# Attention and FFN on one core: an opening emitted step by step, with some of its work on other engines

## The chip, the core and the metric

The kernel runs on one core of a Trainium2 chip. The metric is the device time of one execution in microseconds (us). Five engines run their own instruction streams in order and wait for each other by semaphores: TensorE (PE; its weight loads are PEld), VectorE (DVE), ScalarE (ACT), GpSimd (POOL), and SyncE (SP), which here issues most of the DMAs. A line such as L166 is a line of the kernel.

## The reference

```
k_p = k.reshape(B, H, S // 8, 8, D).mean(axis=3);  v_p likewise     # B=8, H=8, S=576, D=64
scores = q @ k_p.T / 8;  attn = softmax(scores);  x = attn @ v_p
x -> (B, S, 512)
xn = (x - mean) / sqrt(var + 1e-6) * g_ln
out = x + relu(xn @ w_ch1) @ w_ch2                                    # 512 -> 2048 -> 512
```

All of it is float32. Keys and values are averaged over eight neighbours before the attention, so each query sees 72 keys.

## The kernel before

The 4608 tokens are cut into 36 tiles of 128, and four tiles make a chunk (nine chunks, c = 0 to 8). A tile has a stage A (load the queries, `scores`, `probs`) and a stage B (`values`: attention output x, its row statistics, the centred and scaled z, and z's split and transpose). A chunk then has the input half of the FFN (`ffn_in`, 16 feature blocks f, hidden values in `ring`) and the output half (`ffn_out`, L765), in two halves over the features and four tiles each.

The FFN runs in f16 with every f32 factor split in a high and a low part, and three products for each factor pair. For that the weights have to be prepared once. W1 and W2 come as 8 blocks each of 128 x 1024 values. For each block `convert` (C) takes a maximum on VectorE (L195), two passes on ScalarE (L198, L202) and one on VectorE (L205). `max_w1` and `max_w2` (M1, M2) turn four blocks' maxima into a scale by way of a small product on TensorE (L149). `split_w` (S) then writes the high part on ScalarE (L161) and the low part on VectorE (L166).

The opening (`START`) prepares the weights and does chunks 0 and 1. Batch 0's and batch 1's keys and values are pooled by products with a banded matrix (L356, L372); later batches' on GpSimd (L299 to L303, L313 to L315). Chunk 0 turns its probabilities and z by products on TensorE (L484, L491, L504), later chunks by DMA. From chunk 2 on the input half uses seven products in place of eight on sums of W1's blocks (`sums_w` T, `sum_last` U: L272 to L276 and L259, L260) and of z.

`START` is a list of steps, traced in that order. The instructions of each engine are then ordered by the framework's scheduler, which runs its own model of the engines' times. So the list sets priorities, not the order in which an engine executes. Buffers: three PSUM tiles for FFN results (`ps_f`), one each for scores, values and small products (`ps_m`); weight blocks land in `tsp`, `ring` and `raw`, keys in two `kr` buffers, values in two `vr` buffers, and a load waits until its buffer is free.

Of the kernel before, what the change touches and what calls it, by code (L numbers as in the profile page):

```python
# [63 lines left out]
def attn_ffn_kernel(ctx: ExitStack, tc: tile.TileContext, qT, kT, v, kvn, kvt, g, w1, w2, out):  # L64
# [78 lines left out]
    def all_max(src, n=P):  # L143


        e, dst = scalar_tile("rowmax"), scalar_tile("allmax")
# [2 lines left out]
        nc.tensor.matmul(  # L149
            ps,  # L150
            lhsT=e.bitcast(BF16)[:n, 1:2].broadcast_to([n, P]),
            rhs=ident[:n, :n],
            start=True,
            stop=True,
        )
        nc.vector.tensor_reduce(out=dst, in_=ps, axis=AX.X, op=ALU.max)
        return dst

    def split(src, scale, hi, lo, shared=False):
# [6 lines left out]
        nc.vector.scalar_tensor_tensor(  # L166
# [21 lines left out]
    def convert(mat, b):  # L188
# [6 lines left out]
        nc.vector.tensor_reduce(  # L195
            out=wm[mat][:, b : b + 1], in_=hi.bitcast(F32), axis=AX.X, op=ALU.max, apply_absolute_value=True
        )
# [7 lines left out]
        nc.vector.scalar_tensor_tensor(  # L205
# [52 lines left out]
    def split_t(src, dst):  # L258
        nc.scalar.copy(out=dst[:, 0], in_=src)  # L259
        nc.gpsimd.tensor_tensor(out=dst[:, 1], in0=src, in1=dst[:, 0], op=ALU.subtract)  # L260

    def sums_w(h, k):
# [54 lines left out]
    def max_v(b):  # L317
# [12 lines left out]
    def tokens(b, n):  # L330
        if (b, n) == (1, 1):
            part = zts[:, 8:16].rearrange("p a c -> p (a c)").bitcast(F32)
            part = part.rearrange("p (i c) -> p i c", i=NTOK - 1)
            return [part[:, i] for i in range(NTOK - 1)] + [at(2, 5 * WC + NTOK * DM, 1)[:, 0]]
        x = at(*((1, 5 * WC), (2, 0), (2, 5 * WC))[2 * b + n], NTOK)
        return [x[:, i] for i in range(NTOK)]

    def load_tokens(b, n):
        x = tokens(b, n)
        if (b, n) == (1, 1):  # L340
            full = zts[:, 8:16].rearrange("p a c -> p (a c)").bitcast(F32)
        else:
            full = area[(1, 2, 2)[2 * b + n]][:, (5, 0, 5)[2 * b + n] * WC :][:, : (NTOK - 1) * DM]
        full = full.rearrange("p (i c) -> p i c", i=NTOK - 1)
        nc.sync.dma_start(out=full, in_=kvn[b, n])
        nc.sync.dma_start(out=x[NTOK - 1][: S % P], in_=kvt[b, n])
# [556 lines left out]
```

## Time and profile before

| what | value |
|---|---|
| median of 3 runs | 871.95 us (871.56 to 872.1) |
| the profiled execution | 870.89 us |
| its span, first to last instruction | 868.8 us |
| mean granted TensorE clock | 0.978 |
| PE busy in the span | 831.3 us |
| DMA, mean over the span | 101 GB/s; 355 to 383 GB/s in the first three of 40 slices |

A profile row of the timeline has start, length, engine, line, operation, output<-input, count, and in brackets the idle time of the engine before it with what ended it. A row of a group has the busy time of all its instructions, the mean of one in ns, and the idle time before them. Up to the end of chunk 1, at about 275 us, the trace shows the opening; behind it chunks 2 to 8.

### The profile page before, as it was taken

To read this page: it belongs to the slowest core of one execution; us is meant where nothing else is said; L and a number is where in the kernel's file an instruction comes from. 1 tells how busy PE (TensorE), PEld (TensorE's weight loads), DVE (VectorE), ACT (ScalarE), POOL (GpSimd) and SP (SyncE) were. 2 spreads that over 40 slices of the span, in tenths; PEclk is the share of its full clock that TensorE was granted. 3 is DMA by queue.
4 is the path that set the end of the run, shared out by engine and by line. 5 is a ranking of instruction groups with operands and counts; after the bars stand their busy time and mean duration, and the time that the engine had idled before them with its cause. 6 is when DMAs were issued, how large, how long until landed. Compare 5 with 4: busy or idle time off the path is not lost. (4 is left out here: it accounts for less than half of the span.)

```text
span 868.8 us, 14907 instructions
## 1 busy us (share of the span) xinstructions
PE 831.3 (96%) x5808; PEld 545.2 (63%) x5808; DVE 561.1 (65%) x1148; ACT 324.3 (37%) x615; POOL 294.9 (34%) x429
## 2 busy tenths in 40 slices
PE   6699896999999999999999998999999999999998
PEld 5586642444556766676676665766766676757483
DVE  4999799814486738574956485648674847494242
ACT  3797442303142424252434332523343333323140
POOL 0534688534465453255213334231111201120000
PEclk9888897999999999999999999999999999999999
DMA  9992520343346342435343414432434143221001
GB/s 355 364 383 77 124 67 7 101 99 71 88 115 170 77 98 63 123 91 121 69 115 89 101 50 123 110 63 49 116 71 65 32 115 62 38 55 55 0 2 48
DMA packets 145109, 87.35 MB, mean 101 GB/s; under 512 B 125328, under 2 KB 126480, under 8 KB 142480
## 3 DMA queue, kind: packets, MB, share of 16 engines
q1 hardware_dynamic: 143888, 85.52, 37.1%
q10 hardware_dynamic: 1152, 0.90, 0.4%
q8 instruction: 45, 0.74, 0.3%
q14 instruction: 24, 0.20, 0.1%
HBM read 45.09 MB, written 9.44 MB: 63 GB/s over the span
## 5 line engine op out<-in xcount | busy, mean ns | idle before, releaser
L765 PE MATMUL ps_f<-w,ring 128*128 128x512 f16 x1728 | 380.7, 379 | 0.0
L765 PEld LDWEIGHTS <-ring 128*128 128x128 f16 x1728 | 167.8, 98 | 193.9 <-issue 0.2
L700 PE MATMUL ps_f<-zts,w 128*128 128x256 f16 x1680 | 207.1, 273 | 3.2 <-DVE raw L721 1.5
L700 PEld LDWEIGHTS <-w 128*128 128x128 f16 x1680 | 163.3, 98 | 23.9 <-issue 2.8
L775 DVE SCALAR_TENSOR_TENSOR x<-ps_f,cy,x 128x512 f32<-128x512 f32 x72 | 53.8, 748 | 124.7 <-PE ps_f L765 122.4
L669 PE MATMUL ps_f<-zts,w 128*128 128x512 f16 (+1 forms) x480 | 96.2, 360 | 9.4 <-DVE x L775 6.6
L700 PE MATMUL ps_f<-zts,tsp 128*128 128x256 f16 x672 | 96.1, 272 | 1.5 <-DVE rowmax L127 1.2
L464 POOL TENSOR_TENSOR phl<-e,phl 128x512 f16<-128x512 f32 x32 | 37.4, 1169 | 159.5 <-ACT phl L457 159.5
L741 DVE SCALAR_TENSOR_TENSOR ring<-raw,ring 128x512 f16<-128x512 f32 x112 | 82.2, 760 | 9.0 <-ACT ring L740 8.7
L740 ACT ACTIVATE ring<-raw 128x512 f16<-128x512 f32 x112 | 64.8, 622 | 54.4 <-DVE raw L734 53.9
L669 PEld LDWEIGHTS <-w 128*128 128x128 f16 x480 | 49.3, 104 | 50.3 <-issue 16.8
L718 ACT COPY raw<-ps_f 128x256 f32<-128x256 f32 x56 | 20.8, 371 | 143.7 <-PE ps_f L700 140.8
L700 PEld LDWEIGHTS <-tsp 128*128 128x128 f16 x672 | 64.0, 98 | 12.1 <-issue 1.9
L638 POOL TENSOR_TENSOR hl<-raw,hl 128x640 f16<-128x640 f32 x28 | 41.0, 1479 | 78.9 <-ACT hl L637 43.0
L734 DVE TENSOR_TENSOR raw<-ps_f,raw 128x256 f32<-128x256 f32 x112 | 42.3, 419 | 22.4 <-PE ps_f L700 22.0
L313 POOL TENSOR_TENSOR vr<-vr 72x256 f32<-72x256 f32 x48 | 38.8, 816 | 48.3 <-DMA vr<-in_v_dram 48.2
L721 DVE TENSOR_TENSOR raw<-ps_f,raw 128x256 f32<-128x256 f32 x56 | 23.7, 424 | 45.6 <-PE ps_f L700 40.5
L453 ACT ACTIVATE e<-e 128x576 f32<-128x576 f32 x32 | 21.8, 683 | 62.6 <-DVE e L441 44.5
L427 PE MATMUL ps_a<-kblk,q 128*128 128x144 f32 (+1 forms) x320 | 44.7, 292 | 0.0
L427 PEld LDWEIGHTS ps_a<-kblk,q 128*128 128x128 f32 (+1 forms) x320 | 40.5, 183 | 5.7 <-issue 2.0
L727 DVE TENSOR_TENSOR raw<-ps_f,raw 128x256 f32<-128x256 f32 x56 | 23.6, 421 | 31.4 <-PE ps_f L700 28.5
L637 ACT CAST hl<-raw 128x640 f16<-128x640 f32 x28 | 19.2, 722 | 57.8 <-DVE a L614 26.3
(137 smaller groups left out, 1000.5 us busy)
## 6 DMA issues: line engine op xcount, KB each, us to landing
q<-in_qT_dram SPq DMA_DIRECT2D x36, 256.0 KB
out_dram<-x SPq DMA_DIRECT2D x36, 256.0 KB
tsp<-in_w_dram SPq DMA_DIRECT2D x8, 1024.0 KB
kr<-in_kT_dram SPq DMA_DIRECT2D x24, 288.0 KB
vr<-in_v_dram SPq DMA_DIRECT2D x48, 144.0 KB
raw<-in_w_dram SPq DMA_DIRECT2D x6, 1024.0 KB
w<-in_kvn_dram SPq DMA_DIRECT2D x3, 1024.0 KB
ring<-in_w_dram SPq DMA_DIRECT2D x2, 1024.0 KB
```

The costliest lines, as they stand in the source:

```text
L313: eng.tensor_add(out=vr[:, 0:4, :], in0=vr[:, 0:4, :], in1=vr[:, 4:8, :])
L427: nc.tensor.matmul(ps[r, p // 2, p % 2 * 2 * KV : (p % 2 + 1) * 2 * KV], lhsT=q[:, p, r], rhs=kblk[b % NKB][:, p, :], start=True, stop=True,)
L464: nc.gpsimd.tensor_tensor(out=ph[:, 0, :, KA:P], in0=e[:, :, 0:KA], in1=ph[:, 0, :, 0:KA], op=ALU.subtract)
L638: nc.gpsimd.tensor_tensor(out=zhl[:, 1, :], in0=src, in1=zhl[:, 0, :], op=ALU.subtract)
L669: nc.tensor.matmul(ps, lhsT=w[:, part, fs], rhs=zT[:, kz, cols], start=(n == 0), stop=(n == 3 * NKT - 1),)
L700: nc.tensor.matmul(ps, lhsT=w[:, part, f * P : (f + 1) * P], rhs=z, start=start and n == 0, stop=stop and n == 3 * KH - 1, skip_group_chec ...
L721: nc.vector.tensor_tensor(out=cc[:, 0, :HC], in0=m2, in1=cc[:, 0, :HC], op=ALU.add)
L734: nc.vector.tensor_tensor(out=cc[:, j, HC:], in0=u3, in1=cc[:, j, HC:], op=ALU.add)
L740: nc.scalar.activation(out=hh[:, 0, f], in_=cc[:, j], func=AF.Relu)
L741: nc.vector.scalar_tensor_tensor(out=hh[:, 1, f], in0=cc[:, j], scalar=0.0, in1=hh[:, 0, f], op0=ALU.max, op1=ALU.subtract)
L765: nc.tensor.matmul(ps, lhsT=h[:, part, i, cols], rhs=w[:, wp, j], start=(n == 0), stop=(n == 3 * NFT // 2 - 1),)
L775: nc.vector.scalar_tensor_tensor(out=x, in0=ps, scalar=out_scale(c, tt, half), in1=x, op0=ALU.mult, op1=ALU.add)
```

## The change

Every operation of the opening becomes a generator that yields where another engine's result is wanted next. `START` now has 574 steps, each naming an operation that is advanced by one piece, and the region runs under `manual_schedule`, so that each engine executes its instructions in exactly the order in which the pieces emit them. Behind the opening the scheduler orders as before. With it, six things move:

- W2's maxima (`MAXM`): in place of VectorE's maximum a ScalarE pass over the converted block writes the sum of absolute values, which bounds the maximum.
- W2's first four low parts (`LO_POOL`): ScalarE scales the block once more in place, and GpSimd subtracts over 128 x 1024.
- Chunk 0's z (`parts_turned`): x is turned by four f32 products, and a fifth product with the negated identity takes the mean off in PSUM; ScalarE reads it twice with z's scale (high part, and all of z), and GpSimd subtracts (`Z_LO`). VectorE's z (L567) and its low part (L507) are gone for chunk 0.
- Chunk 1's z is computed by GpSimd.
- Batch 1's keys and values are pooled on GpSimd like those of the later batches (HK.1, HV.1), from loads into `kr` and `vr`.
- Batch 0's keys (K0) are summed by VectorE from a load in the later batches' layout. Small memsets of `split_v` go to GpSimd.

```diff
+MAXM = {1: "dve", 2: "act"}
+LO_POOL = ((2, 0), (2, 1), (2, 2), (2, 3))
+Z_LO = "pool"
 START = """
-LD K0 A.0 C.1.0 V0 R.2.0 R.2.1 C.1.1 A.1 C.1.2 B.0 C.1.3 M1.0 S.1.0 S.1.1 S.1.2 S.1.3 R.2.2 R.2.3 B.1 A.2 I.0.0.0 ...
+LN.2 LN.2 LK.0 LK.0 LK.1 LK.1 Q.0 Q.0 R.1.0 R.1.0 R.1.1 R.1.1 Q.1 Q.1 R.1.2 R.1.2 LG LG HK.1.0 A.0 R.1.3 R.1.3 HV.1.0
...
-    def split(src, scale, hi, lo, shared=False):
+    def split(src, scale, hi, lo, pool=False):
         nc.scalar.activation(out=hi, in_=src, func=AF.Copy, scale=scale)
-        if shared:
-            nc.gpsimd.tensor_scalar_mul(out=src, in0=src, scalar1=scale)
+        if pool:
+            nc.scalar.activation(out=src, in_=src, func=AF.Copy, scale=scale)
+            yield
             nc.gpsimd.tensor_tensor(out=lo, in0=src, in1=hi, op=ALU.subtract)
             return
+        yield
         nc.vector.scalar_tensor_tensor(
...
+        if MAXM[mat] == "act":
+            yield
+            nc.scalar.activation(
+                out=lo.bitcast(F32), in_=w, func=AF.Abs, accum_out=wm[mat][:, b : b + 1]
+            )
...
-    def parts_turned(z, dst):
-        ps = psum["ps_f"].tile([P, CH], F32, name="ps_f")
+    def parts_turned(x, ln, cv, dst):
+        ps = psum["ps_m"].tile([P, CH], F32, name="ps_m").rearrange("p (k c) -> p k c", k=NKT)
         for k in range(NKT):
-            nc.tensor.transpose(out=ps[:, k * P : (k + 1) * P], in_=z[:, k * P : (k + 1) * P], identity=identf)
-        ps = ps.rearrange("p (k c) -> p k c", k=NKT)
-        nc.scalar.copy(out=dst[:, 0:NKT], in_=ps)
-        nc.vector.tensor_tensor(out=dst[:, NKT:], in0=ps, in1=dst[:, 0:NKT], op=ALU.subtract)
+            nc.tensor.matmul(ps[:, k], lhsT=x[:, k * P : (k + 1) * P], rhs=identf, start=k == 0, ...)
+        nc.tensor.matmul(ps, lhsT=ln[:, 0:1].broadcast_to([P, P]), rhs=minus.unsqueeze(1).broadcast_to([P, NKT, P]), ...)
+        yield
+        scale = cv[:, 1:2]
+        nc.scalar.activation(out=dst[:, 0:NKT], in_=ps, func=AF.Copy, scale=scale)
+        if Z_LO == "pool":
+            z = wk1.tile([P, DM], F32, name="z").rearrange("p (k c) -> p k c", k=NKT)
+            nc.scalar.activation(out=z, in_=ps, func=AF.Copy, scale=scale)
+            yield
+            nc.gpsimd.tensor_tensor(out=dst[:, NKT:], in0=z, in1=dst[:, 0:NKT], op=ALU.subtract)
+            return
...
-        nc.vector.tensor_scalar(
+        (nc.gpsimd if c < 2 else nc.vector).tensor_scalar(
             out=z, in0=x, scalar1=ln[:, 0:1], scalar2=ln[:, 2:3], op0=ALU.subtract, op1=ALU.mult
         )
...
     def first_k():
-        pool_tokens_k(0)
+        for i in range(2):
+            if i:
+                yield
+            kr = k_first[:, 2 * i : 2 * i + 2]
+            nc.vector.tensor_add(out=kr[:, :, 0:4], in0=kr[:, :, 0:4], in1=kr[:, :, 4:8])
+            nc.vector.tensor_add(out=kr[:, :, 0:2], in0=kr[:, :, 0:2], in1=kr[:, :, 2:4])
+            for j in range(2):
...
-    for token in START.split():
-        name, *args = token.split(".")
-        ops[name](*map(int, args))
+    begun = {}
+    with tc.manual_schedule():
+        for token in START.split():
+            if token not in begun:
+                name, *args = token.split(".")
+                begun[token] = iter(ops[name](*map(int, args)) or ())
+            next(begun[token], None)
+        for steps in begun.values():
+            all_of(steps)
```

The lines shift: L166 becomes L211, L205 becomes L264, L195 becomes L248 (W1 only), L161 is L204, L765 is L882.

VectorE before, from the scale of W1's first half (`gs`) on; `w_91` is W1, `w_92` W2, `x` and `z` are tiles 0 and 1:

```order
L231 TENSOR_SCALAR gs<-g_sb,s_323 128x4
L546 TENSOR_TENSOR x<-ps_a,rs 128x512
L557 BN_STATS st<-x 128x6
L166 SCALAR_TENSOR_TENSOR w_91<-w_91,gs 128x1024
L558 BN_AGGR ln<-st 128x2
L536 TENSOR_SCALAR sm<-ps_a,cv 128x8
L567 TENSOR_SCALAR z<-x,ln 128x512
L544 RECIPROCAL rs<-sm 128x8
L546 TENSOR_TENSOR x<-ps_a,rs 128x512
L166 SCALAR_TENSOR_TENSOR w_91<-w_91,gs 128x1024
L557 BN_STATS st<-x 128x6
L507 TENSOR_TENSOR zts<-ps_f,zts 128x4x128
```

VectorE in the change at the same place:

```order
L297 TENSOR_SCALAR gs<-g_sb,s_320 128x4
L264 SCALAR_TENSOR_TENSOR w_91<-w_91,ring 128x1024
L511 TENSOR_REDUCE mx<-ps_a 128x8
L264 SCALAR_TENSOR_TENSOR w_92<-w_92,raw 128x1024
L211 SCALAR_TENSOR_TENSOR w_91<-w_91,gs 128x1024
L264 SCALAR_TENSOR_TENSOR w_91<-w_91,ring 128x1024
L211 SCALAR_TENSOR_TENSOR w_91<-w_91,gs 128x1024
L641 TENSOR_SCALAR sm<-ps_a,cv 128x8
L649 RECIPROCAL rs<-sm 128x8
L651 TENSOR_TENSOR x<-ps_a,rs 128x512
```

z and its low part are gone from VectorE, the low parts of W1 stand between conversions, and tile 0's x now stands ahead of `gs`.

GpSimd before, from the last probabilities of chunk 0 (`pt`) to tile 4's (`phl`); `kr` and `kblk` are keys of batch 2:

```order
L497 TENSOR_TENSOR pt<-phl_116,pt 72x512 x2
L456 MEMSET phl_116 128x8x40
L299 TENSOR_TENSOR kr<-kr 128x288
L300 TENSOR_TENSOR kr<-kr 128x144
L303 TENSOR_TENSOR kblk_113<-kr 64x72 x4
```

GpSimd in the change, from the low part of tile 3's z (L605) to W2's first low parts (L208):

```order
L605 TENSOR_TENSOR zts<-z,zts 128x4x128
L385 TENSOR_TENSOR vr<-vr 72x256
L386 TENSOR_TENSOR vr<-vr 72x128
L387 TENSOR_TENSOR vp<-vr 72x64
...
L371 TENSOR_TENSOR kr<-kr 128x288
L372 TENSOR_TENSOR kr<-kr 128x144
L375 TENSOR_TENSOR kblk_113<-kr 64x72 x2
L208 TENSOR_TENSOR w_92<-w_92 128x1024
```

W2's low parts stand behind all of batch 1's value heads (`vr`), its key pairs and one key pair of batch 2.

SP before, from W1's last two blocks of the first half (`ring`) on:

```order
L186 DMA ring<-in_w_dram 128x2048 x2
L419 DMA q<-in_qT_dram 128x512
L186 DMA raw<-in_w_dram 128x2048 x2
L345 DMA w_92<-in_kvn_dram 128x2048
L346 DMA w_92<-in_kvt_dram 64x512
```

SP in the change, from W2's second block (`raw`) on:

```order
L231 DMA raw<-in_w_dram 128x2048
L366 DMA kr<-in_kT_dram 128x576
L379 DMA vr<-in_v_dram 72x512
L231 DMA tsp_93<-in_w_dram 128x2048
L366 DMA kr<-in_kT_dram 128x576
L493 DMA q<-in_qT_dram 128x512
L231 DMA tsp_94<-in_w_dram 128x2048
L379 DMA vr<-in_v_dram 72x512
L231 DMA raw<-in_w_dram 128x2048
```

Loads of weight blocks now alternate with loads into the two key and two value buffers.

More of the change, by code (lines that the diff above doesn't have):

```diff
@@ L328, in at, with tokens, load_tokens @@
         return area[m][:, lo : lo + n * DM].rearrange("p (i c) -> p i c", i=n)
[L330 to L346, printed above, removed]
+    def tokens(n):
+        if n == 1:
+            part = zts[:, 8:16].rearrange("p a c -> p (a c)").bitcast(F32).rearrange("p (i c) -> p i c", i=NTOK - 1)
+            return part, at(2, 5 * WC + NTOK * DM, 1)[:, 0]
+        x = at(*((2, 5 * WC), None, (1, 5 * WC))[n], NTOK)
+        return x[:, : NTOK - 1], x[:, NTOK - 1]
+    def load_tokens(n):
+        full, last = tokens(n)
+        nc.sync.dma_start(out=full, in_=kvn[n])
+        nc.sync.dma_start(out=last[: S % P], in_=kvt[n])
     def token_tiles():
@@ L367, in pool_tokens_v @@
     def pool_tokens_v(b):
-        x = tokens(b, 1)
+        full, last = tokens(2 if b == 0 else 1)
+        x = [full[:, i] for i in range(NTOK - 1)] + [last]
         ps = psum["ps_m"].tile([P, DM], F32, name="ps_m")[:KV]
@@ new lines, in probs_turned @@
+        for n in range(4):
+            h = 4 * i + n
+            nc.tensor.matmul(
+                ps[:, n],
+                lhsT=kblk[0][:, h // 2, h % 2 * KV : (h % 2 + 1) * KV],
+                rhs=q[:, h // 2],
+                start=True,
+                stop=False,
+            )
+            nc.tensor.matmul(
+                ps[:, n], lhsT=mx[:, h : h + 1].broadcast_to([P, KV]), rhs=minus, start=False, stop=True
+            )
+        yield
+        hs = slice(4 * i, 4 * i + 4)
+        nc.scalar.activation(out=et[:KV, hs], in_=ps, func=AF.Exp, scale=EXP_SCALE)
@@ L515, in values @@
             cv = scalar_tile("cvm", 3)
-            for r, b in segs:
-                nc.vector.tensor_copy(out=cv[r], in_=CV[b][r])
         pt = PT.pop(t)
@@ L535, in values @@
                 )
+        yield
+        if len(segs) > 1:
+            for r, b in segs:
+                nc.vector.tensor_copy(out=cv[r], in_=CV[b][r])
         nc.vector.tensor_scalar(
@@ L566, in values @@
         Z[t] = ln
-        nc.vector.tensor_scalar(
+        if not seven:
+            yield
+        nc.gpsimd.tensor_copy(out=ln[:, 2:4], in_=cv[:, 1:3])
+        if c == 0:
+            zTs[c] = zts[:, c * 8 : (c + 1) * 8]
+            yield
+            yield from parts_turned(x, ln, cv, zTs[c][:, :, tt * P : (tt + 1) * P])
+            return
+        if seven:
+            yield
+        (nc.gpsimd if c < 2 else nc.vector).tensor_scalar(
             out=z, in0=x, scalar1=ln[:, 0:1], scalar2=ln[:, 2:3], op0=ALU.subtract, op1=ALU.mult
@@ L784, in stage_a, with stage_b @@
             load_q(t + 2)
-        scores(t)
-        probs(t)
-    def stage_b(t):
-        values(t)
-        transpose_z()
+            yield
+        yield from scores(t)
+        if t >= TPC:
+            yield
+            yield from probs(t)
+    def stage_b(t, turn=True):
+        yield from values(t)
+        if turn and t >= TPC:
+            yield
+            transpose_z()
     def prep_k(b, parts=range(NPAIR)):
```

251 lines of the change are left out of this document (166 added, 85 removed).

## The prediction, made before the run

> **What bounds the kernel now.** I read the busy row and the slices of the page first, then busy time by stretches, then TensorE's timeline.
>
> ```profile
> PE 831.3 (96%) x5808; PEld 545.2 (63%) x5808; DVE 561.1 (65%) x1148; ACT 324.3 (37%) x615; POOL 294.9 (34%) x429
> DVE  4999799814486738574956485648674847494242
> ```
> ```profile
> 20.00:50.00 30.00, 20.37 (x165) 17.10 (x164) 29.33 (x54) 24.63 (x30) 12.04 (x16) 0.77 1.02 366
> 50.00:105.00 55.00, 49.80 (x406) 39.41 (x405) 50.23 (x111) 38.45 (x58) 27.03 (x38) 0.88 0.56 185
> 105.00:164.00 59.00, 51.37 (x266) 24.53 (x264) 56.26 (x71) 21.21 (x31) 49.54 (x46) 0.91 0.20 44
> ```
> ```profile
> 180.00:200.00 20.00, 20.00 (x98) 9.75 (x97) 5.70 (x9) 3.59 (x7) 1.28 (x2) 1.00 0.32 85
> ```
>
> The columns of a stretch are its length, then busy time of PE, PEld, DVE, ACT and POOL, TensorE's granted clock, and the DMA share and rate. The share of 96% hides two regimes. In the 20 us from 180 TensorE is never idle and runs at clock 1.00, while VectorE has 14 us free. From 20 to 164 us VectorE is busy 135.8 of 144 us, and TensorE runs at 0.77 to 0.91 with gaps. So the opening is bound by VectorE's queue, and all behind it by TensorE. What the change can move is the point at which the second regime begins.
>
> ```profile
> 51.95 4.09 PE L669 MATMUL ps_f<-zts,w 128*128 128x256 f16 x36
> ...
> 107.46 20.88 PE L765 MATMUL ps_f<-w,ring 128*128 128x512 f16 x96
> ```
> ```profile
> 134.10 4.44 PE L669 MATMUL ps_f<-zts,w 128*128 128x512 f16 x12 [3.17 <-DVE x L775]
> ...
> 164.39 20.88 PE L765 MATMUL ps_f<-w,ring 128*128 128x512 f16 x96
> ...
> 228.09 1.14 PE L427 MATMUL ps_a<-kblk,q 128*128 128x144 f32 x8
> 229.07 0.19 PE L532 MATMUL ps_a<-va,pt 128*128 128x65 f16 x1
> ...
> 229.59 7.93 PE L669 MATMUL ps_f<-zts,w 128*128 128x512 f16 x36
> ```
>
> These rows (start, length, instruction, count) give three marks: the first FFN product at 51.95, the first output product **t0** at 107.46, and the second output half **t1** at 164.39. Behind t1 stand 868.8 - 164.39 = 704.4 us, which I call R. So span = t1 + R, and I have to find the new t1.
>
> **The change part by part.** R first. Counted in the order of the changed kernel, 12 score products stand between the two output halves where 4 stood before, so 8 fewer stand behind t1. Four take 1.14 us (row of 228.09), 8 take 2.2. R becomes 702.2, if nothing behind t1 starts to wait.
>
> From t0 to t1 TensorE's own work is 96 output products (20.9), 96 input products (36 take 7.93, so 21.1), 12 scores (3.3) and 48 value products (16 stand between 229.07 and 229.59, so 1.6), in sum 46.9 us. Before, the stretch took 56.9 with 2.2 less in it, so 12.2 us were lost to waits such as the quoted 3.17 for an eviction by VectorE and to the lower clock.
>
> Now t0. The first output half needs the high and low parts of W2's first four blocks, and it comes after all of chunk 0's first two input quarters. Three queues lead there; I add up each in the changed order.
>
> ```profile
> 6.14 8.78 PE L356 MATMUL ps_m<-zts,w 128*128 128x16 f32 x40 [6.14 <-DMA w<-in_kvn_dram]
> 18.24 4.63 PE L372 MATMUL ps_m<-w,zts 128*72 128x512 f32 x10
> ```
> ```profile
> 10.04 1.12 ACT L198 ACTIVATE w<-tsp 128x1024 f32<-128x1024 f32 x1 [7.96 <-DMA tsp<-in_w_dram]
> ...
> 21.61 1.16 ACT L198 ACTIVATE w<-ring 128x1024 f32<-128x1024 f32 x1 [0.28 <-DMA ring<-in_w_dram]
> ```
> ```profile
> L202 ACT ACTIVATE tsp<-tsp 128x1024 int32<-128x1024 uint16 x8 | 9.1, 1135 | 0.0
> L677 ACT ACTIVATE ring<-ps_f 128x256 f16<-128x256 f32 x16 | 5.7, 370 | 2.8 <-PE ps_f L669 2.8
> L495 ACT ACTIVATE phl<-ps_f 72x512 f32<-72x512 f32 x8 | 4.6, 581 | 1.4 <-PE ps_f L491 1.4
> ```
>
> ScalarE. In 10.04 us the loads brought 2.5 MB (keys, a query tile, one weight block), in 21.61 us 7.1 MB: 2.5 us for each MB. In the new order W1's first block ends at 3.7 MB, so at about 13 us. From there ScalarE has, up to the last scaled copy of W2's first half, 36 passes over 128x1024 (20 conversions, 4 + 4 high parts, 4 scaled copies, 4 maxima) at 1.14 = 41.0, 16 halves of probabilities at 0.6 = 9.6, 8 reads of the turned z at 0.58 = 4.6, 14 Relu over 256 columns at 0.37 = 5.2, and about 5.5 for the two value splits and two tiles' exponentials: 65.9. Its work ends at 13 + 66 = **79**. Back to back these passes overlap by about 0.1, so 72 is the other end. A maximum with an accumulator is not in the trace: from below it is a plain pass, 1.14, from above a pass and a small one more (0.37 as for 256 columns); I take the plain one, and 8 x 0.37 = 3 us is kept for the range.
>
> ```profile
> L313 POOL TENSOR_TENSOR vr<-vr 72x256 f32<-72x256 f32 x26 | 22.1, 860 | 20.6 <-DMA vr<-in_v_dram 20.5
> L314 POOL TENSOR_TENSOR vr<-vr 72x128 f32<-72x128 f32 x26 | 15.8, 619 | 0.2
> L299 POOL TENSOR_TENSOR kr<-kr 128x288 f32<-128x288 f32 x14 | 12.9, 921 | 26.2 <-DMA kr<-in_kT_dram 26.1
> L464 POOL TENSOR_TENSOR phl<-e,phl 128x512 f16<-128x512 f32 x11 | 12.7, 1153 | 20.4 <-ACT phl L457 20.4
> L260 POOL TENSOR_TENSOR tsp<-raw,tsp 128x512 f16<-128x512 f32 x8 | 12.4, 1564 | 0.0
> ...
> L497 POOL TENSOR_TENSOR pt<-phl,pt 72x512 f16<-72x512 f32 x8 | 10.9, 1365 | 39.0 <-ACT pt L496 39.0
> L303 POOL TENSOR_TENSOR kblk<-kr 64x72 f32<-64x72 f32 x24 | 10.2, 423 | 9.6 <-PE ps_a L427 6.2 <-PE ps_f L484 2.3
> L315 POOL TENSOR_TENSOR vp<-vr 72x64 f32<-72x64 f32 x26 | 9.3, 370 | 3.2 <-DVE ln L558 1.3 <-DVE a L615 1.0 <-DVE vb L166 0.8
> L638 POOL TENSOR_TENSOR hl<-z,hl 128x512 f16<-128x512 f32 x7 | 9.1, 1300 | 7.2 <-ACT hl L637 7.1
> L300 POOL TENSOR_TENSOR kr<-kr 128x144 f32<-128x144 f32 x14 | 8.4, 610 | 0.3
> ```
>
> GpSimd gets the largest share. Up to W2's fourth low part it has 9 value heads at 0.86 + 0.62 + 0.37 = 1.85 (16.7), 5 key pairs at 0.92 + 0.61 + 2 x 0.42 = 2.38 (11.9), 8 probability halves at 1.37 (10.9), 4 low parts of z at 1.3 (5.2), 2 tiles' low parts (3.2), copies and memsets (2), and the 4 new subtractions over 1024 elements. Those are not in the trace: twice a pass over 512 is 2.3 (L464) to 3.1 (L260). I take 2.6, 10.4 in all. Sum 60.3. Its first input, tile 0's probabilities, comes about 19.5 us in, since values' loading ends at 6.1, the pooling products take 4.6 and ScalarE's first copies and conversions follow. Its new waits are for ScalarE's copies of z: behind each of the four stand batch 1's poolings and then W2's low parts, for which the output products wait, but by the order ScalarE has z ready when GpSimd comes to it. So GpSimd ends at **80**; the fourth subtraction is needed only in the last quarter of the first output tile, 4 us after t0.
>
> ```profile
> L436 DVE TENSOR_REDUCE mx<-ps_a 128x8 f32<-128x576 f32 x15 | 11.2, 749 | 5.0 <-PE ps_a L427 2.7 <-PE ps_m L149 2.2
> L166 DVE SCALAR_TENSOR_TENSOR w<-w,gs 128x1024 f16<-128x1024 f32 x8 | 11.9, 1486 | 0.0
> L205 DVE SCALAR_TENSOR_TENSOR w<-w,tsp 128x1024 int32<-128x1024 int32 x8 | 9.7, 1212 | 1.0 <-ACT tsp L202 1.0
> ...
> L195 DVE TENSOR_REDUCE wm<-tsp 128x1 f32<-128x1024 f32 x8 | 9.6, 1204 | 7.4 <-DMA tsp<-in_w_dram 7.4
> L557 DVE BATCH_NORM_STATS2 st<-x 128x6 f32<-128x512 f32 x14 | 9.6, 688 | 0.2
> L567 DVE TENSOR_SCALAR z<-x,ln 128x512 f32<-128x512 f32 x12 | 8.4, 700 | 0.7
> ...
> L678 DVE SCALAR_TENSOR_TENSOR ring<-ps_f,ring 128x256 f16<-128x256 f32 x16 | 6.4, 407 | 0.0
> ```
>
> VectorE. Off its queue go 8 maxima (9.6), 4 of W2's low parts (4 x 1.49 = 6.0), chunk 0's z and its low part (8 x 0.7 = 5.6) and chunk 1's z (2.8): 24.0 us. On it come batch 0's key sums, bounded by 576 elements at 0.75 and two shorter halvings, 3.5, at a time when it waits for loads. Up to the last 256-column product's eviction it has 8 maxima (9.6), 10 conversions (12.1), 4 low parts (5.9), 10 passes over scores (7.5), 5 tiles' values at two passes of 0.69 and 0.59 of short ones (9.8), 16 evictions (6.5), the key sums and some 13 of small ones: 68. From 9 us that ends at **77**, with the waits for ScalarE that I see in the order (W1's low parts stand directly behind its high parts) at about 79.
>
> TensorE loses batch 0's key products (8.8 us, row of 6.14) and batch 1's poolings, and gets per tile of chunk 0 four turning products for the transposes and one of 512 columns in f32 (ten records took 4.63, so 0.9). That is costed at nothing, since ScalarE sets the pace there; without that cover it would be 3.7 us at most.
>
> All three end at 77 to 80, and TensorE's own work ahead of t0 does too. W1's fourth low part frees the first FFN product: ScalarE has 19 of its long passes and 10 us of short ones up to the fourth high part, 13 + 31.7, and the low part takes 1.5, which gives 46 instead of 51.95. Behind it stand 192 products of 256 columns (36 take 4.09, so 21.8) and about 11 us of attention, which ends at 79. I take t0 = 80. From there VectorE's queue to W2's last low part holds 48 us (8 low parts 11.9, 6 conversions 7.3, 6 passes over scores 4.5, 2 tiles' values 3.9, 12 evictions of 512 columns at about 0.7, 8.5, and some 12 of short ones and first sums of W1), TensorE's 46.9. Of the old loss of 12.2 I keep half, since the four output evictions still stand between low parts: t1 = 80 + 46.9 + 5.6 = 132.5. Span = 132.5 + 702.2 = 834.7. The profiled execution took 870.89, 2.1 more than its span and 1.1 less than the median of 871.95; so 834.7 + 2.1 + 1.1 = **838**.
>
> The sums of W1 that went behind t1 cost nothing while VectorE has room there (14 of 20 us free in the row of 180). GpSimd's queue to the last of them adds up to 178 us by the rows above; 19.5 + 178 = 198, and chunk 2, which needs them, starts about 108 us behind t1, at 240. Were that cover gone, each us past 240 would be one us of the time.
>
> **A rule weighed.**
>
> ```profile
> 26.13 1.16 POOL L497 TENSOR_TENSOR pt<-phl,pt 72x512 f16<-72x512 f32 x1 [24.03 <-ACT pt L496]
> ...
> 51.65 2.01 POOL L497 TENSOR_TENSOR pt<-phl,pt 72x512 f16<-72x512 f32 x1 [8.79 <-ACT pt L496]
> ```
> ```profile
> 117.50 2.45 DVE L242 TENSOR_TENSOR ws<-f,s 128x1 f32<-128x1 f32 x1
> ```
>
> One GpSimd pass takes 1.16 us or 2.01, and a VectorE product of one element took 2.45 us while GpSimd was busy. So the two engines hold each other up here. [...]
>
> **The rivals.** (a) *The engines take turns.* Undisturbed, GpSimd's 60.3 us would be about 60.3 x 1.16 / 1.37 = 51; beside them VectorE has 19.6 us of passes with two inputs in SBUF (10 conversions, 4 low parts, 2 value splits at 0.8). If all of it is serial, GpSimd ends at 19.5 + 70.6 = 90.1, and the next stretch loses as much as before: t1 = 90.1 + 46.9 + 12.2 = 149.2, time **855**. For it: the 2.01. Against: the mean of 1.37 has such waits in it. (b) *Every queue overlaps as its short ends allow.* t0 = 76, no loss but 1.5: t1 = 124.4, time **830**. (c) *GpSimd's fixed order makes it slower.* The loads of W2's and W1's later blocks now stand on SP's queue behind loads into the key and value buffers, which GpSimd must first free; each delay of GpSimd then delays weights, too. It decides when t1 passes 164.4 + 2.2, so when GpSimd takes over 94 us for the 60. At the worst ratio seen (2.01 / 1.16 = 1.73) it takes 104: t0 = 124, t1 = 176, time **881**. Against: that ratio is rare in the rows. (d) *The gain is given back behind t1*, by GpSimd at chunk 2: 42 us of slack speak against it.
>
> **How the numbers follow.** Forecast 838, with 834 to 846 as its own range: 0.50. (b) 0.18, (a) up to 858: 0.20, between (a) and the old time 0.05, (c) 0.05, no change 0.02. The range leaves out what lies beyond (a) and below (b): 828 to 857. What the measurement of this kernel can tell from no change is about 0.2%; faster by more 0.93, the same 0.02, slower 0.05.
>
> **What would show it.** Right: first FFN product near 46, t0 near 80, t1 near 130 to 135, GpSimd over 80% busy from 20 to 80 us, and some 700 us behind t1. TensorE waiting for GpSimd at the fourth W2 block, with GpSimd passes near 2 us, would show (a); weight loads that land behind value loads while ScalarE waits for them, (c). The prediction is wrong at its root if R is not near 702, or if ScalarE, now the fullest engine up to t0, waits for long stretches in its fixed order.

## The result, and the profile after

| | before | after |
|---|---|---|
| median of 4 runs each, side by side | 872.03 us (871.56 to 874.86) | 841.67 us (839.94 to 843.9) |
| ratio after / before | | 0.9647, 95% interval 0.9615 to 0.9678 |
| first FFN product | 51.95 us | 50.03 us |
| first output product, t0 | 107.46 us | 84.79 us |
| second output half, t1 | 164.39 us | 132.52 us |
| the rest, R (span less t1) | 704.4 us | 708.1 us |

The kernel became 30 us faster; 838 us was forecast. t1 came where it was forecast (132.5), but not by the forecast's steps: t0 came 4.8 us late, and the stretch behind it was 4.8 us shorter. R was 5.9 us longer. Here and below, medians and ratios are of runs at the usual clock; one run of e4 below, 1058.23 us at a clock of 0.754, is not in them.

The first rows of the page after, busy time and VectorE's and GpSimd's slices:

```profile
PE 809.4 (96%) x5742; PEld 527.5 (63%) x5742; DVE 545.3 (65%) x1110; ACT 339.1 (40%) x636; POOL 347.0 (41%) x497
DVE  5988997674767476746764686559555856484242
POOL 1898989684777442444225162402110211020000
```

GpSimd is now 8 or 9 tenths busy in every slice from the second to the seventh (21 to 147 us), as VectorE is in the second to the sixth. Three rows of the table by stretches (length, then PE, PEld, DVE, ACT, POOL, granted clock, DMA):

```profile
46.00:80.00 34.00, 29.11 (x264) 24.62 (x261) 30.37 (x56) 28.78 (x48) 30.06 (x43) 0.98 0.62 178
80.00:105.00 25.00, 24.18 (x143) 12.33 (x142) 24.00 (x44) 20.01 (x23) 22.91 (x23) 0.96 0.60 212
105.00:140.00 35.00, 33.77 (x208) 17.75 (x206) 32.17 (x49) 25.44 (x38) 32.09 (x36) 1.00 0.65 149
```

Four engines are 85 to 89% busy from 46 to 80 us, and from 80 to 140 us TensorE is never short of work for long, at a clock of 0.96 to 1.00. Before, it ran at 0.88 from 50 to 105 us and at 0.91 from there to 164. The marks in TensorE's timeline:

```profile
50.03 6.71 PE L784 MATMUL ps_f<-zts,w 128*128 128x256 f16 x60
...
84.79 20.88 PE L882 MATMUL ps_f<-w,ring 128*128 128x512 f16 x96
...
132.52 15.70 PE L882 MATMUL ps_f<-w,ring 128*128 128x512 f16 x72
...
242.88 0.81 PE L817 MATMUL ps_f<-zts,w 128*128 128x256 f16 x6 [1.34 <-DVE x L893]
244.20 0.50 PE L817 MATMUL ps_f<-zts,w 128*128 128x256 f16 x3 [0.51 <-DMA zts<-hl]
245.58 4.12 PE L817 MATMUL ps_f<-zts,w 128*128 128x256 f16 x21 [0.88 <-DMA zts<-hl]
...
387.12 0.82 PE L817 MATMUL ps_f<-zts,w 128*128 128x256 f16 x6 [2.63 <-DVE rowmax L168]
```

The last four rows show waits that grew, at the start of chunk 2 and at one later place. Part of why t0 is late shows in two timelines, GpSimd's and VectorE's, at the same moments:

```profile
70.96 2.13 POOL L208 TENSOR_TENSOR w<-w 128x1024 f16<-128x1024 f32 x1
...
80.23 2.13 POOL L208 TENSOR_TENSOR w<-w 128x1024 f16<-128x1024 f32 x1 [2.51 <-ACT w L206]
```
```profile
71.13 3.04 DVE L264 SCALAR_TENSOR_TENSOR w<-w,raw 128x1024 int32<-128x1024 int32 x1
...
80.36 2.03 DVE L284 TENSOR_SCALAR wm<-wm 128x4 int32<-128x4 int32 x1
```

A conversion that took 1.21 us before takes 3.04 us: it begins 0.17 us after GpSimd's low part, which ends at 73.09, and then needs 1.08 more. A pass over four columns takes 2.03 us and ends when GpSimd's next low part does (82.36). That four-column pass stands in the chain of W1's second scale, whose small product stands on TensorE ahead of the first output product, with one tile's scores between them; TensorE waited 0.82 us for it. From 40 us to t0 TensorE waited 9.4 us in sum, and all but 0.3 of that for VectorE; it never waited there for W2's low parts from GpSimd.

### The profile page after: what moved, and what is told of

Read it like the earlier page. It is cut to its first block, busy times and chain, and to the rows that moved or that the text cites. A ratio compares the mean times of both kernels' runs of the same rounds, so it can differ in the third digit from the quotient of the medians.

```text
span 840.6 us, 14847 instructions
## 1 busy us (share of the span) xinstructions
PE 809.4 (96%) x5742; PEld 527.5 (63%) x5742; DVE 545.3 (65%) x1110; ACT 339.1 (40%) x636; POOL 347.0 (41%) x497
## 4 chain that ended last, share of the span: by engine, by line
PE 70%; DVE 10%; POOL 9%; DMA 4%; issue 3%; ACT 2%; ACTq 0%; SPq 0%; POOLq 0%; DVEq 0%
PE ps_f L882 34%; PE ps_f L817 25%; PE ps_f L784 5%; PE ps_a L501 3%; DMA vr<-in_v_dram 2%; POOL vr L385 2%; POOL vr L386 1%; DVE w L264 1%; POOL vp L387 1%; POOL kblk L375 1%; PE ps_m L441 1%; POOL pt L575 1%; PE ps_a L633 1%; DVE w L211 1%; PE ps_a L634 1%
## 5 line engine op out<-in xcount | busy, mean ns | idle before, releaser
L882 PE MATMUL ps_f<-w,ring 128*128 128x512 f16 x1728 | 380.7, 379 | 0.0
L882 PEld LDWEIGHTS <-ring 128*128 128x128 f16 x1728 | 167.7, 98 | 193.8 <-issue 0.2
L784 PE MATMUL ps_f<-zts,w 128*128 128x512 f16 (+1 forms) x480 | 87.0, 340 | 3.2 <-DVE ring L795 2.4
L385 POOL TENSOR_TENSOR vr<-vr 72x256 f32<-72x256 f32 x56 | 50.0, 898 | 34.3 <-DMA vr<-in_v_dram 34.0
L753 POOL TENSOR_TENSOR hl<-z,hl 128x512 f16<-128x512 f32 x18 | 21.5, 1196 | 36.0 <-ACT hl L751 22.7
```

What stands on the lines that cost most here:

```text
L385: eng.tensor_add(out=vr[:, 0:4, :], in0=vr[:, 0:4, :], in1=vr[:, 4:8, :])
L753: nc.gpsimd.tensor_tensor(out=zhl[:, 1, :], in0=src, in1=zhl[:, 0, :], op=ALU.subtract)
L784: nc.tensor.matmul(ps, lhsT=w[:, part, fs], rhs=zT[:, kz, cols], start=(n == 0), stop=(n == 3 * NKT - 1),)
L882: nc.tensor.matmul(ps, lhsT=h[:, part, i, cols], rhs=w[:, wp, j], start=(n == 0), stop=(n == 3 * NFT // 2 - 1),)
```

## The experiments

All ratios are against runs of the kernel before on the same chip. Marks are from each run's profiled execution, in us.

| run | what | FFN | t0 | t1 | R | median | ratio, interval |
|---|---|---|---|---|---|---|---|
| e1_sched | moved work, order by the scheduler | 49.23 | 99.05 | 167.42 | 713.2 | 884.19 | 1.0130 (1.0110, 1.0151) |
| e2_back | fixed order, moved work back | 56.86 | 94.39 | 152.40 | 704.6 | 860.48 | 0.9863 (0.9836, 0.9889) |
| e3_pool_less | 2 of 3 sums of batch 1 left out | 45.62 | 80.71 | 129.12 | 708.7 | 838.34 | 0.9612 (0.9587, 0.9637) |
| e4_tail | end of the list reordered | 50.28 | 85.08 | 132.79 | 707.5 | 839.85 | 0.9625 (0.9604, 0.9646) |
| e5_lo_back | W2's low parts back | 50.83 | 84.83 | 134.20 | 706.4 | 842.97 | 0.9676 (0.9650, 0.9703) |
| e6_max_back | W2's maxima back | 50.46 | 87.06 | 138.38 | 707.2 | 848.50 | 0.9728 (0.9698, 0.9759) |
| e7_z_back | z back | 53.67 | 91.92 | 141.21 | 710.7 | 850.65 | 0.9753 (0.9732, 0.9773) |
| e8_front_tail | front and end reordered | 56.07 | 90.78 | 138.51 | 710.9 | 850.06 | 0.9749 (0.9729, 0.9768) |
| e9_front2 | front alone, mended | 46.29 | 86.52 | 133.43 | 707.9 | 843.17 | 0.9660 (0.9639, 0.9681) |
| e10_tail3 | end, W1's last sums by VectorE | 50.84 | 85.59 | 133.29 | 705.8 | 840.91 | 0.9642 (0.9622, 0.9663) |
| e11_both | e9 and e10 | 46.25 | 86.49 | 133.34 | 709.2 | 844.18 | 0.9677 (0.9655, 0.9699) |
| e12_z_back_psf | e7, other buffer | 50.98 | 86.93 | 135.63 | 706.8 | 843.69 | 0.9680 (0.9618, 0.9743) |

**Order or moved work (e1, e2).** e1 takes the fixed order away, e2 takes the moved work back (chunk 0's products for z and the pooling of both batches stay as changed):

```diff
-    with tc.manual_schedule():
+    with ExitStack():
```
```diff
-MAXM = {1: "dve", 2: "act"}
-LO_POOL = ((2, 0), (2, 1), (2, 2), (2, 3))
-Z_LO = "pool"
+MAXM = {1: "dve", 2: "dve"}
+LO_POOL = ()
+Z_LO = "dve"
...
-        (nc.gpsimd if c < 2 else nc.vector).tensor_scalar(
+        nc.vector.tensor_scalar(
```

> The changed kernel with the same list and the same moved work, but the order of each engine in the opening is left to the scheduler again. If the moved work carries the gain (24 us off VectorE's queue, of which the opening was short), the time stays within 842 to 848 and the first output product stays near 85 us. If the fixed order carries a part of it, ScalarE and VectorE serve W1 and W2 in another order, the first output product comes at 90 to 100 us, and the time is 850 to 858. I expect 850.

> The fixed order alone: VectorE takes back W2's maxima (8 x 1.2), W2's first four low parts (4 x 1.49 to 1.7), chunk 0's low parts of z and chunk 1's z, some 22 us, in the same list. In 46 to 80 us VectorE was busy 30.4 of 34 us, so it has some 4 us of room ahead of the first output product. If moved work carries the gain: the first output product at 92 to 98, time 850 to 862. If the order alone carries it: 842 to 846. I expect 855.

With the moved work and the new list, but without the fixed order, the kernel is slower than before, by 1.3%; with the fixed order, but without the three moves of e2, it gains 1.4%; the whole change gains 3.5%. The fixed order over exactly the old work was not run. Neither theory of e1 had that. TensorE's and GpSimd's timelines of e1 show a part of the cause:

```profile
106.93 9.76 PE L882 MATMUL ps_f<-w,ring 128*128 128x512 f16 x32 [5.63 <-POOL w L208]
```
```profile
86.59 3.10 POOL L208 TENSOR_TENSOR w<-w 128x1024 f16<-128x1024 f32 x1 [1.44 <-ACT w L206]
...
104.76 2.12 POOL L208 TENSOR_TENSOR w<-w 128x1024 f16<-128x1024 f32 x1
...
117.46 3.16 POOL L208 TENSOR_TENSOR w<-w 128x1024 f16<-128x1024 f32 x1
...
129.86 2.13 POOL L208 TENSOR_TENSOR w<-w 128x1024 f16<-128x1024 f32 x1
```

The scheduler fills GpSimd with the sums of later keys and values between W2's four low parts. They end at 132 us instead of 86.9, and the output products wait 7.2 us for them (5.63 and 1.54). That is not all of it: the first output product itself comes at 99.05, 14.3 us later than in the changed kernel, before any of these waits, and behind it TensorE waits 8.2 us more for VectorE (4.75 and 3.42). What made t0 late in e1 was not followed further. So GpSimd's room helps only if its queue has the urgent passes first.

In e2 VectorE was busy 22.48 of 34 us from 46 to 80, so the amount of its work does not explain 860 by itself. The table of TensorE's waits up to 140 us (total, times, longest) has another cause at its head:

```profile
PE ps_m L582 <- DVE zts L608: 11.7, 3, 6.8
```

**Which of the moves (e5, e6, e7, e12).** Each takes back a part of e2's diff: e5 `LO_POOL`, e6 `MAXM`, e7 `Z_LO` and the last line. e12 is e7 with another buffer in `parts_turned`:

```diff
-        ps = psum["ps_m"].tile([P, CH], F32, name="ps_m").rearrange("p (k c) -> p k c", k=NKT)
+        ps = psum["ps_f"].tile([P, CH], F32, name="ps_f").rearrange("p (k c) -> p k c", k=NKT)
```

> The changed kernel, with W2's first four low parts on VectorE again (4 x 1.49 us more there, four scaled copies of 1.14 fewer on ScalarE, four passes of 2.13 fewer on GpSimd). VectorE has 3.6 of 34 us free from 46 to 80, so if VectorE's queue sets the start of the output half, it comes 2 to 4 us later and the time is 843 to 847. If GpSimd's or ScalarE's queue sets it, the output half starts no later: 839 to 842. I expect 844.

> The changed kernel, with W2's maxima on VectorE again, and ahead of each block's ScalarE passes (8 x 1.2 us more on VectorE, four of them ahead of the first output product; 8 x 1.34 fewer on ScalarE). By the length of VectorE's queue alone, 4.8 us less 3.6 free: first output product 1 to 3 us later, time 843 to 846. If the place counts more than the length (ScalarE's in-order queue then waits for a VectorE maximum that stands behind low parts), it is 5 to 10 us later, time 847 to 852. I expect 847.

> The changed kernel, with chunk 0's low parts of z on VectorE, read from PSUM (4 x 0.7 us), and chunk 1's z on VectorE (0.55 in place of GpSimd's 2.16 us); ScalarE loses four copies of 0.68, GpSimd four passes of 1.16 and four of 2.16. In the run with all moved work back, TensorE's turning products waited 11.7 us for VectorE's reads of the one buffer that they share. If that is so by itself, the first FFN product comes 3 to 6 us after 50.0 and the time is 844 to 848. If it was only VectorE's total work that made those reads late, it comes within 1.5 us of 50.0: 840 to 843. I expect 844.

> As the run with chunk 0's low part of z and chunk 1's z on VectorE, but the turned z lands in one of the three buffers of the FFN results in place of the single one for small products. If the 9 us that this move cost come from the single buffer (TensorE's next turning products waited 10.4 us for VectorE's reads of it, while VectorE was busy only 23.5 of 34 us), most of them go: first FFN product near 51 in place of 53.7, time 842 to 845. If they come from the place of those reads in VectorE's queue, whatever the buffer, the time stays at 849 to 852. If the FFN results now want for a buffer: above 853. I expect 845.

Against 841.67, W2's low parts are worth 1.3 us, which is within the intervals; the maxima 6.8; z 9.0. The three make 17.1 of the 18.8 us that e2 lost. e6's time came as expected, but not its path: t0 is 2.3 us later, not 5 to 10, and the stretch from t0 to t1 is 3.6 us longer, with a wait of 3.66 us for one of VectorE's low parts. z's share is not mainly VectorE's time. e7's timeline of VectorE, and its waits of TensorE:

```profile
38.27 1.59 DVE L211 SCALAR_TENSOR_TENSOR w<-w,gs 128x1024 f16<-128x1024 f32 x1
...
41.73 0.18 DVE L662 BATCH_NORM_AGGREGATE ln<-st 128x2 f32<-128x6 f32 x1
41.83 0.72 DVE L608 SCALAR_TENSOR_TENSOR zts<-ps_m,cv,zts 128x512 f16<-128x512 f32 x1
```
```profile
PE ps_m L582 <- DVE zts L608: 10.4, 3, 5.3
```

VectorE's read of the turned z (L608) stands behind a weight's low part and the next tile's x, and until then the only `ps_m` buffer is taken, so the next tile's turning products wait. With a buffer of `ps_f`, e12 gets 7.0 of the 9.0 us back by the medians. Its trace agrees: of e7's three waits of 5.3, 1.8 and 3.3 us the last two are gone (the first stays, 5.26 us), and t1 comes 5.6 us earlier. So most of what z's move brings seems to be that this buffer comes free early. e12's interval is wide, though: it takes in the changed kernel and reaches into e7's.

**What holds VectorE up (e3).** Two of three sums over batch 1's keys and values are left out on GpSimd:

```diff
+        if b != 1:
             eng.tensor_add(out=kr[:, 0:4, :], in0=kr[:, 0:4, :], in1=kr[:, 4:8, :])
             eng.tensor_add(out=kr[:, 0:2, :], in0=kr[:, 0:2, :], in1=kr[:, 2:4, :])
...
```

The same stands in the pooling of the values (`vr`).

> Left out: the first two of the three sums over batch 1's keys and values on GpSimd (about 8 heads x 1.5 and 4 pairs x 1.5 us, some 18 us), so batch 1 is pooled over two of its eight neighbours only. If VectorE's passes with two inputs in SBUF are held up by GpSimd's passes, L264's mean falls from 1507 and 1848 ns to near 1212 and L211's from 1704 to near 1486, and the first output product comes 3 to 6 us before 84.8: time 836 to 839. If GpSimd's passes do not hold VectorE up, L264 and L211 keep their means, and only what waits for GpSimd itself comes earlier: time 840 to 842. I expect 838.

Two of VectorE's groups in the opening, the changed kernel first, then e3:

```profile
L211 DVE SCALAR_TENSOR_TENSOR w<-w,gs 128x1024 f16<-128x1024 f32 x8 | 13.6, 1704 | 0.1
...
L264 DVE SCALAR_TENSOR_TENSOR w<-w,raw 128x1024 int32<-128x1024 int32 x6 | 11.1, 1848 | 0.0
```
```profile
L211 DVE SCALAR_TENSOR_TENSOR w<-w,gs 128x1024 f16<-128x1024 f32 x8 | 11.7, 1466 | 0.0
...
L264 DVE SCALAR_TENSOR_TENSOR w<-w,raw 128x1024 int32<-128x1024 int32 x6 | 9.9, 1655 | 0.0
```

With the same instructions, VectorE's passes with two inputs in SBUF become shorter when GpSimd does less. L211 falls as far as expected (from 1704 to 1466 ns), L264 only part of the way (from 1848 to 1655, not 1212 ns; over its 16 passes 1509, from 1598), with GpSimd still busy 21.5 of 34 us from 46 to 80. t0 comes 4.1 us earlier, at 80.71, and the first FFN product at 45.62, both close to the forecast's 80 and 46. So GpSimd's load, its own length and what it holds up together, is what made both late; e3 doesn't part the two. Its time lies 3.3 us below the changed kernel's, as forecast, but the two intervals overlap.

**What is lost behind t1 (e4, e10).** The end of the list; `Y.2` is chunk 2's token scales:

```diff
-... B.11 B.11 U.0.0 U.0.0 G.1.2.1 G.1.2.1 B.11 B.11 U.1.1 U.1.1 U.1.0 U.1.0 B.11 B.11
-G.1.3.1 G.1.3.1
+... B.11 B.11 G.1.2.1 G.1.2.1 B.11 B.11 B.11 B.11 U.0.0 U.0.0 U.1.1 U.1.1 U.1.0 U.1.0
+G.1.3.1 G.1.3.1 Y.2
```

> Only the last line of the list: chunk 2's token scales (12 VectorE instructions of 4 columns, three of them 1.08 to 1.41 us long beside GpSimd) are emitted as the opening's last step, so behind the last two evictions, and GpSimd's last sums of W1 behind all low parts of tile 11's z. If the waits of 1.34 (eviction), 0.51 and 0.88 us (transposed z) at 242.9 to 245.6 us come from this order, they go, the clock in 240 to 260 us rises from 0.91 towards 1.00, and what stands behind the second output half falls from 708.1 to 704 to 706 us: time 838 to 840. The rival is that chunk 2 then waits for W1's last sums or its token scales instead: 841 to 843. I expect 839.5.

e10 has `Y.2` too, but puts the six U steps between the second and third piece of V.10 (tile 10's z), and gives their subtraction to VectorE.

> The changed kernel with the end of the list changed: W1's last four sums (L327, 1.15 us each on GpSimd) are subtracted by VectorE ahead of its pass over tile 10's z, where it waited 2.5 us, and chunk 2's token scales stand behind the last eviction. If GpSimd's lateness at the end of the opening causes both the waits at chunk 2's start (2.7 us, and 1.8 us by the clock) and the one for batch 3's maximum at 265 us in the run with only the order changed (1.9 us, and 1.8 by the clock), all of them go, and the stretch behind the second output half falls from 708.1 to 703 to 704.5: time 837 to 838.5. If the waits come back elsewhere: 840 to 842. I expect 838.

In e4's profiled execution chunk 2 starts at 241.73 without a wait, and R falls only by 0.6 us. Most of the loss came back 24 us later. VectorE's timeline there, the changed kernel first, then e4, and e4's timeline of TensorE:

```profile
264.59 0.68 DVE L391 TENSOR_REDUCE mv<-vp 72x1 f32<-72x512 f32 x1 [1.45 <-POOL vp L387]
```
```profile
264.39 0.68 DVE L391 TENSOR_REDUCE mv<-vp 72x1 f32<-72x512 f32 x1 [5.67 <-POOL vp L387]
```
```profile
265.74 0.82 PE L882 MATMUL ps_f<-w,ring 128*128 128x512 f16 x3 [1.87 <-DVE rowmax L168]
```

VectorE takes the maximum of batch 3's pooled values, and TensorE, which has the small product of that maximum in its queue, waits for VectorE. The values come no later than in the changed kernel (264.39 against 264.59): GpSimd ends W1's last sums ahead of them at 242.6 in place of 242.1. What is new is that TensorE and VectorE, no longer held up at 243 us, are there early and wait. So a second limit stood 24 us behind the first, and most of what the first wait had cost is not won. Short waits at two places cost more than their length: the clock was lower behind them (0.66 and 0.68). By stretches, the changed kernel, then e4:

```profile
240.00:245.00 5.00, 2.85 (x27) 1.82 (x26) 4.24 (x6) 0.37 (x1) 4.79 (x8) 1.00 0.74 183
245.00:250.00 5.00, 4.42 (x26) 3.25 (x26) 0.42 (x1) 2.83 (x6) 2.60 (x7) 0.66 0.87 278
```
```profile
265.00:270.00 5.00, 4.09 (x13) 2.06 (x14) 4.86 (x15) 1.08 (x3) 2.49 (x6) 0.68 0.18 59
```

Behind waits of 2.73 us in sum, or of 1.87, the clock was 0.66 or 0.68 for five us, so 1.6 to 1.7 us more are lost, an estimate from these rows. (The wait of 2.63 at 387 us was not followed by such a drop, nor was one of 1.92 at 300 us in e10, with 1.00 behind both; so the length of the wait alone does not decide, and what does stays open.) e4 lost 1.8 us more by the same estimate from 500 to 520 us (0.91; the changed kernel has 1.00). Its profiled execution took 841.97 us at a mean clock of 0.992; three others took 838.2 to 839.9 at 0.997 to 0.998. So these drops do not fall in every execution, and the forecast of 839.5 may be met by the median, 839.85, better than by the trace. e10 lowers R to 705.8, still with waits of 0.3 to 1.9 us at 245, 260, 300 and 509. Its time of 840.91 can't be told from 841.67, nor can e4's 839.85.

**Reordering the front (e8, e9, e11).** e8 has the U steps ahead of V.10's fifth piece, on GpSimd, `Y.2`, and at the front W1's fourth split (`S.1.3`) ahead of tile 1's z and tile 2's x, and tile 1's low part of z ahead of a key pair:

```diff
-... B.1 B.0 B.0 HK.1.1 HK.1.1 B.1 B.2 S.1.2 S.1.2 B.2 B.1 S.1.3 E.3.0 E.3.1 B.1 B.1 HV.1.0 ...
+... B.1 B.0 B.0 B.1 B.2 S.1.2 S.1.2 S.1.3 S.1.3 S.1.3 B.2 B.1 E.3.0 E.3.1 B.1 B.1 HK.1.1 HK.1.1 HV.1.0 ...
```

> The changed kernel with two pieces of the list moved. Front: W1's fourth high part ahead of tile 1's reads of z on ScalarE, its low part ahead of tile 2's x on VectorE, tile 1's low part of z ahead of a key pair on GpSimd. Tail: the last three of W1's sums on GpSimd where it waits (3.3 us at 223.6), and chunk 2's token scales behind the last eviction. Front: the first FFN product near 48 in place of 50.03, the output halves 1.5 to 2 us earlier, if the low part of W1 sets it; if GpSimd's pass over z does, near 49. Tail: no wait of more than 0.3 us within 30 us of chunk 2's start, and no low clock there (2.7 us of waits and 1.8 us of clock). Together 836 to 838; if the waits come back elsewhere behind it, 839 to 841. I expect 837.

It was 8 us slower than the changed kernel. TensorE's timeline, then GpSimd's and VectorE's at another place of it:

```profile
51.82 0.74 PE L501 MATMUL ps_a<-kblk,q 128*64 128x144 f32 x2 [5.36 <-POOL kblk L375]
...
56.07 7.78 PE L784 MATMUL ps_f<-zts,w 128*128 128x256 f16 x60
```
```profile
229.65 3.39 POOL L327 TENSOR_TENSOR w<-raw,w 128x512 f16<-128x512 f32 x3
```
```profile
229.54 3.77 DVE L681 TENSOR_SCALAR raw<-x,ln 128x512 f32<-128x512 f32 x1 [2.50 <-POOL ln L673]
```

Both inputs of the first FFN product were ready at 48.7, but tile 4's scores stand ahead of it on TensorE (and tile 2's turning products behind these), and they need the key pair that I had moved back: one piece moved on one engine, and the wait turned up on another. Later one VectorE pass, 0.55 us in the changed kernel (L681, median), took 3.77 beside three GpSimd passes in a row. e9 moves tile 4's scores and tile 2's turning products behind the first three FFN tiles, without the end's changes; e11 adds e10's:

> The front part of the run before alone, and mended: in it the first FFN products stood on TensorE behind tile 4's scores (5.36 us of wait for a key pair that had been moved back on GpSimd) and behind tile 2's turning products; both are now moved behind the first three FFN tiles. If W1's fourth low part (it ended at 45.7 in that run) and tile 1's low part of z (48.7) are all that stands ahead, the first FFN product comes at 48 to 49 in place of 50.03, the output halves 1 to 2 us earlier, and the time is 839 to 841. If tile 2's later z is missed at the second column half instead: 842 to 845. I expect 840.5.

> Both pieces together: if they add up, 836 to 837.5; if the front's gain is lost behind it, 838. I expect 836.5.

The first FFN product comes at 46.29 (one of them, the rest from 47.74; 48 to 49 was expected), and t0 is no earlier (86.52). The stretch of e9 behind that product:

```profile
45.00:50.00 5.00, 3.95 (x37) 3.00 (x36) 4.74 (x7) 3.47 (x6) 3.62 (x5) 0.50 0.13 52
```

TensorE works there at a clock of 0.50 (1.00 in the changed kernel), which by these figures costs about 2 us, and later it waits for VectorE as before (1.7 us for an eviction, 1.66 for the scale ahead of t0). So an earlier first FFN product does not by itself bring t0 forward. e11, both pieces together, shows the same marks and is no faster than e9 (844.18 against 843.17). No version was found that beats the changed kernel by more than the measurement can tell.

## Why the prediction was right, point by point

The time lies 3.7 us above the forecast and in its range. The mechanism held, but that the number is so near is partly luck: two errors cancelled in t1, and 2.1 of the 5.9 us by which R was longer do not show in the time (the profiled execution was 1.7 us longer than its span and 0.7 above the median, where 2.1 and 1.1 had been added).

- **What bounds the kernel** held: the opening by its preparing queues, the rest by TensorE. "What the change can move is the point at which the second regime begins" (t1) is what happened.
- **The first FFN product** was forecast at 46 and came at 50.03, so 4.0 of t0's 4.8 us were there already; from it to t0 it took 34.8 us against 34 forecast. ScalarE began at 13.3 and did the 19 long passes that were counted, but it waited 3.6 us in between for VectorE and TensorE, for which the sum of 31.7 had no term. So W1's fourth high part ended at 47.4 in place of 44.7. The low part behind it on VectorE was priced at 1.5 us and took 2.15, beside a pass of GpSimd, and its end at 50.04 is where the first FFN product starts. ScalarE's and VectorE's rows:

```profile
46.27 1.14 ACT L204 ACTIVATE w<-w,gs 128x1024 f16<-128x1024 f32 x1
```
```profile
47.89 2.15 DVE L211 SCALAR_TENSOR_TENSOR w<-w,gs 128x1024 f16<-128x1024 f32 x1
```

- **t0 = 80** was 4.8 us early. The priced lengths were good: GpSimd started at 19.6 (19.5 forecast), did 62 us of work against 60.3, and a low part took 2.13 where I took 2.6. GpSimd waited 3.3 us for ScalarE's scaled copies of W2, for which its sum had no term either; but TensorE never waited for the low parts that came of it. What failed is that VectorE's passes were priced at their old means: L264's 16 passes averaged (8 x 1507 + 6 x 1848 + 2 x 1214) / 16 = 1598 ns, not 1212. Ahead of t0, nine of them took 14.6 us in place of 10.9 and W1's four low parts 7.2 in place of 5.9, so 5.0 us more, about as much as t0 is late. That is rival (a)'s mechanism, at a part of its price: it would have given t0 near 90. That just its 19.6 us of passes with two SBUF inputs take turns with GpSimd no run shows: in e3 such passes became shorter with less work on GpSimd (L211 from 1704 to 1466 ns, L264 from 1848 to 1655), but neither long pass that stood out beside GpSimd, L284 with 2.03 us here and L681 with 3.77 in e8, is one of them.
- **The stretch from t0 to t1**: its work of 46.9 us was near (46.5 without the waits), "of the old loss of 12.2 I keep half" was not. It took 47.7 us, a loss of 0.8. In the fixed order TensorE waited there for one low part (0.8) and one maximum (0.4), and for no eviction. Besides, half of 12.2 is 6.1, where the sum has 5.6: by its own words it would have given t1 = 133.0 and 838.5. This error and t0's cancel; t1 = 132.5 was right by their sum, not by its steps.
- **R = 702.2** "if nothing behind t1 starts to wait": something did. R was 5.9 us longer. Up to chunk 2 TensorE's work shrank by 1.9 of the 2.2 forecast. Against that stand a wait of 1.34 us ahead of chunk 2, 2.4 more us of waits behind it (0.51 + 0.88 + 0.79 + 2.63 + 0.48 + 1.52 + 0.32 = 7.1, against 1.21 + 0.34 + 1.34 + 1.52 + 0.32 = 4.7 before) and the 1.7 us of clock, in sum 5.4; with the 0.3 that was not saved that is 5.7 of the 5.9. The step that failed is rival (d)'s "42 us of slack". W1's sums do not end at 198 but at 242, because the fixed order puts the last of them between low parts of z and because GpSimd waits in it. What TensorE waited for there was not these sums, though, but an eviction and transposed z; e4, which reorders the end, takes these waits away.
- **Rival (c)**, that a fixed order makes GpSimd slower, had it the wrong way round: e1 shows that without it the kernel is slower than before. Its sign did not come either: ScalarE waited for no weight load from 13 us on. That the moved work costs time without the order was no case of mine.
- **The accumulating maximum** was taken as a plain pass. e1's timeline of ScalarE prices it: start to start 1.03 + 0.09 us, beside 1.05 (51.43 to 52.48) for a plain pass, so the plain price was good to 0.07 us.

```profile
49.80 1.15 ACT L274 ACTIVATE tsp<-w 128x1024 f32<-128x1024 f32 x1
50.83 0.20 ACT L274 ACTIVATION_READ_ACCUMULATOR tsp<-w 128x1 f32 x1
50.92 0.62 ACT L573 CAST pt<-phl 72x512 f16<-72x512 f32 x1
51.43 1.16 ACT L256 ACTIVATE w<-raw 128x1024 f32<-128x1024 f32 x1
52.48 1.13 ACT L260 ACTIVATE raw<-raw 128x1024 int32<-128x1024 uint16 x1
```

- TensorE's extra 3.7 us, costed at nothing, were not tried by themselves.

## What to carry to other kernels

Here, moving work to an engine with room paid only when its queue had the urgent passes first: with the moved work under the scheduler's order the kernel lost 12 us against before, and under a fixed order three of these moves are worth 19 us. When a pass is moved, look at which single buffer it frees and who stands behind it in order, not only at the busy time it takes along. Before a wait is taken away, look at what the engine will meet next: e4 only reached the next limit sooner. And where two errors of a sum can cancel, check the marks between its terms before calling the sum understood.

## What the runs showed of the hardware

- VectorE passes with one tensor input were long beside GpSimd's, too. L681 took 0.55 us in the changed kernel (median of 28), and in e8 once 3.77 (229.54 to 233.31 us) beside three GpSimd passes (229.65 to 233.04). L284, over four columns, took 0.17 us in the changed kernel at 27.3 us, and 2.03 (80.36 to 82.39) beside one low part of GpSimd (80.23 to 82.36). That a VectorE pass lasts about as long as three GpSimd passes running is shown by e8's rows alone.
- Waits of TensorE of 2.73 us in sum (changed kernel, 243 us) and of 1.87 (e4, 266 us) were followed by five us at a clock of 0.66 and 0.68; waits of 2.63 (387 us) and 1.92 (e10, 300 us) were followed by 1.00. What parts the two pairs no run here shows.
- GpSimd's `tensor_scalar` over 128x512 in f32 (chunk 1's z, L681) took 2.07 us at its shortest in the changed kernel, its subtraction of the same size (L605) 1.15 in the mean.
